# Head loads on one queue, q tiles and normaliser spread over the state stage, folded Wo written group by group

## The chip, the cores and the metric

One core of one Trainium2 chip. The metric is the time of one execution in device microseconds; "span" is the profiled part of one profiled execution, about 1.7 us shorter. TensorE is called PE (its weight loads PEld), VectorE DVE, ScalarE ACT, SyncE (which issues the DMAs) SP, GpSimd POOL.

## The reference

Linear attention with 32 heads of 20 channels over 2048 tokens, model width 640, then an output projection:

```python
qkv = (x @ wqkv) -> q, k, v            # x 2048x640, wqkv 640x1920, bf16
phi = lambda t: where(t > 0, t + 1, exp(t)) + 1e-6
kv  = einsum("bhsd,bhse->bhde", phi(k), v)
z   = einsum("bhsd->bhd", phi(k))
num = einsum("bhqd,bhde->bhqe", phi(q), kv)
den = einsum("bhqd,bhd->bhq", phi(q), z)[..., None] + 1e-6
out = (num / den) @ wo
```

The kernel never forms v. It accumulates the state P = x^T phi(k), makes kv = wv^T P per head, and folds kv into Wo: W2 = blockdiag(kv) Wo. Then out = (phi(q) / den) W2, one matmul chain for each of 16 token tiles.

## The kernel before

The stages on PE, in order: a **head** (loads, transposes of the first x tiles), **k** (16 token tiles, then phi(k)), the **state** (two halves of 16 steps), then a **late stage** (kv, six "w2 groups" that make W2, most q tiles, den and its spread, the normaliser), then the **output** tiles. Here den makes the denominators of a block of four token tiles, the spread brings their inverses to the columns of phi(q), and the normaliser multiplies phi(q) by them. W2 comes out of its matmuls with rows grouped by head, while the output matmuls need it in another row order. This kernel brings the rows to other partitions by DMA, so W2 makes a round trip: copied to SBUF (`w2g`), written to a DRAM scratch (`w_rows`), read back as `w2p`. No output matmul can start before all of `w2p` is there.

```python
        def w2_rows():
            P.add("sp", lambda e: e.dma_start(
                w2d[0:5 * GW, :].rearrange("(g p) n -> p g n", p=GW),      # GW = 120
                w2g[0:GW, 0:5 * D].rearrange("p (g n) -> p g n", n=D)),
                reads=[("w2g", g) for g in range(5)], writes=["w2d"], dma=True)
            P.add("sp", lambda e: e.dma_start(
                w2d[5 * GW:D, :], w2g[0:gsz[5], 5 * D:6 * D]), ...)
            for c in range(NC_):                                           # 5 reads, 128 partitions each
                P.add("sp", lambda e, c=c: e.dma_start(
                    w2p[:, c * D:(c + 1) * D],
                    w2d.rearrange("(h c j) n -> c h j n", c=NC_, j=4)[c]),
                    reads=["w2d", "w2d5"], writes=[("w2p", c)], dma=True)
...
        for h in range(2):                       # state: 3 q tiles in each half
            for st in range(NT):
                p_step(h, st)
                ...
                if st == 7:
                    next_q(5 + qi[0] % 3)
            p_out(h)
            next_q(5 + qi[0] % 3)
            next_q(5 + qi[0] % 3)
        ...
        kv_group(0)                              # late stage: 14 q tiles
        next_q(5)
        z_finish(4)
        w2_group(0, 2)
        next_q(6)
        w2_group(1, 0)
        den(0, 4)
        ...                                      # a q tile between any two w2 groups
        w2_group(5, 0)
        den(1, 4)
        w2_rows()
        ...                                      # 8 more q tiles, den and normaliser of blocks 1 and 2
        for st in range(2):
            out_tile(st)
        ...
```

A q tile is five matmuls on PE (1.085 us), then one ACT instruction and two DVE instructions; its PSUM bank is free after the last of these.

## Time and profile before

| | before |
|---|---|
| median of the first runs (range) | 109.37 us (109.25 to 109.81) |
| span of the profiled run | 107.7 us |
| PE busy | 92% |
| PE waits over 0.2 us, all together | 4.9 us |
| first w2 group to first output matmul | 61.3 to 81.0 us: 19.7 us |
| `w2p` complete (landing record of the last read) | 79.7 us |

The page of the profile: span, busy shares, PE's busy tenths in 40 slices, and the clock granted to PE in the same slices (9 is full).

```profile
span 107.7 us, 1890 instructions
PE 99.6 (92%) x749; PEld 64.8 (60%) x755; DVE 68.2 (63%) x136; ACT 41.3 (38%) x77; POOL 10.7 (10%) x27
PE   5899999999799999999999999985999879999990
PEclk9999999999999999999999999999999999999999
```

PE is busy nearly everywhere: the kernel is bound by the matmuls, and there is little to win but the holes. The four longest waits of PE by releaser (total us, times, longest) name them:

```profile
PE ps L323 <- DVE pq L336: 1.5, 1, 1.5
PE ps L261 <- DVE eps L155: 1.3, 1, 1.3
PE ps L482 <- ACT rd L466: 0.7, 1, 0.7
PE ps L297 <- DVE pk L288: 0.7, 1, 0.7
```

L323 is a q tile waiting for a PSUM bank, L297 the first state matmul waiting for the banks of the k tiles, L482 an output tile waiting for the PSUM bank from which ACT copies the last spread. In the timeline of PE and of SP (start, duration, engine, line, operation, what ended the idle time before it) the round trip looks like this:

```profile
61.32 0.46 PE L413 MATMUL ps<-wog,kvt 120*120 120x320 bf16 x2
...
71.89 0.39 PE L462 MATMUL ps<-rdc,em 128*128 128x128 bf16 x4
73.80 3.41 PE L323 MATMUL ps<-xT,wqp 128*128 128x512 bf16 x14 [1.52 <-DVE pq L336]
...
81.00 2.88 PE L482 MATMUL ps<-w2p,pq 128*128 128x320 bf16 x20
```

```profile
68.91 0.34 SPq L423 DMA_DIRECT2D w_rows<-w2g  x1
70.25 0.29 SPq L427 DMA_DIRECT2D w_rows<-w2g  x1
74.43 3.16 SPq L431 DMA_DIRECT2D w2p<-w_rows  x5
```

The five reads again, with the starts of the first and the last, and then the page's line of their median time to landing (last figure, us):

```profile
L431 SPq DMA_DIRECT2D w2p<-w_rows x5: 587/603/604, 74.4 to 77.0; - x5
w2p<-w_rows SPq DMA_DIRECT2D x5, 160.0 KB, 2.7
```

The writes are issued at 68.9 and 70.3, the reads from 74.4, the last read lands at 79.7. So the trip takes 10.8 us from the first write's issue and 18.4 us from the first w2 group (61.3). PE spends 19.7 us on the w2 groups and other work (waits of 1.5 us included) before it wants W2, and L482 starts at 81.0 without a wait. There are 1.3 us to spare.

### The profile page before, as it was taken

What the parts mean: (1) busy time and instruction counts of PE and PEld (TensorE: products, weight loads), DVE (VectorE), ACT (ScalarE), POOL (GpSimd) and SP (SyncE); (2) the same over time, 40 slices, a digit from 0 to 9 for tenths busy, and PEclk for the clock granted to TensorE, in tenths of its full rate; (3) what the DMA queues carried; (4) which work ended last, traced back from release to release, by engine and by line L of the source; (5) the groups of instructions that cost most, each with busy time, mean ns of one, the idle gap of its engine ahead of it and who ended that gap; (6) DMA issues with size and microseconds to landing.
All of it is one profiled execution on the core that took longest, in us unless ns stands there. A gap on an engine that the chain in (4) does not pass through costs nothing.

```text
span 107.7 us, 1890 instructions
## 1 busy us (share of the span) xinstructions
PE 99.6 (92%) x749; PEld 64.8 (60%) x755; DVE 68.2 (63%) x136; ACT 41.3 (38%) x77; POOL 10.7 (10%) x27
## 2 busy tenths in 40 slices
PE   5899999999799999999999999985999879999990
PEld 2467777777476674676767745432446557777760
DVE  1216998888899899701236674999879583333331
ACT  0404555555500206202035289872665433333330
POOL 6881000191000000000000000000000000000000
PEclk9999999999999999999999999999999999999999
DMA  2998999999980000000000000082730222333333
GB/s 52 370 203 190 223 145 213 383 366 363 266 161 0 0 3 0 0 0 6 0 0 3 0 0 6 14 215 75 194 111 0 85 104 85 119 117 125 118 120 115
DMA packets 16330, 12.24 MB, mean 114 GB/s; under 512 B 8386, under 2 KB 16322, under 8 KB 16322
## 3 DMA queue, kind: packets, MB, share of 16 engines
q1 hardware_dynamic: 15602, 11.31, 38.6%
q10 hardware_dynamic: 720, 0.82, 2.2%
q8 instruction: 6, 0.10, 0.4%
q14 instruction: 2, 0.02, 0.1%
HBM read 6.72 MB, written 3.44 MB: 94 GB/s over the span
## 4 chain that ended last, share of the span: by engine, by line
PE 75%; DVE 13%; ACT 5%; DMA 3%; issue 1%
PE ps L270 19%; PE ps L482 18%; PE ps L297 15%; PE ps L323 15%; DVE za L342 4%; DVE pq L336 3%; DMA xn<-in_x_dram 3%; ACT eq L331 3%; PE ps L199 2%; DVE pq L473 2%; PE ps L441 2%; PE ps L392 1%; DVE eq L333 1%; ACT rd L466 1%; PE ps L373 1%
## 5 line engine op out<-in xcount | busy, mean ns | idle before, releaser
L323 PE MATMUL ps<-xT,wqp 128*128 128x512 bf16 x94 | 22.9, 379 | 1.8 <-DVE pq L336 1.5
L297 PE MATMUL ps<-pk,xn 128*128 128x320 bf16 x160 | 22.4, 299 | 0.8 <-DVE pk L288 0.7
L482 PE MATMUL ps<-w2p,pq 128*128 128x320 bf16 x160 | 22.2, 299 | 0.7 <-ACT rd L466 0.7
L270 PE MATMUL ps<-wk,xT 128*128 128x320 bf16 x160 | 22.3, 299 | 0.0
L297 PEld LDWEIGHTS ps<-pk,xn 128*128 128x128 bf16 x160 | 15.5, 98 | 7.9 <-DVE pk L288 1.0
L331 ACT ACTIVATE eq<-ps 128x512 bf16<-128x512 f32 x20 | 11.9, 597 | 21.4 <-PE ps L323 21.3
L482 PEld LDWEIGHTS ps<-w2p,pq 128*128 128x128 bf16 x160 | 15.5, 98 | 7.0 <-ACT rd L466 0.8
L270 PEld LDWEIGHTS ps<-wk,xT 128*128 128x128 bf16 x160 | 15.7, 98 | 6.4 <-issue 0.6
L283 ACT ACTIVATE ek<-ps 128x640 bf16<-128x640 f32 x16 | 11.2, 704 | 13.5 <-PE ps L270 13.5
L323 PEld LDWEIGHTS ps<-xT,wqp 128*128 128x128 bf16 x100 | 9.3, 98 | 11.0 <-DVE pq L336 1.9
L491 DVE CAST osb<-ps 128x320 bf16<-128x320 f32 x16 | 7.8, 490 | 11.5 <-PE ps L482 11.5
L336 DVE SCALAR_TENSOR_TENSOR pq<-ps,eq 128x512 bf16<-128x512 f32 x20 | 13.8, 692 | 0.7
L288 DVE SCALAR_TENSOR_TENSOR pk<-ps,ek 128x640 bf16<-128x640 f32 x16 | 13.2, 825 | 0.5
L333 DVE TENSOR_SCALAR eq<-eq 128x512 bf16<-128x512 bf16 x20 | 5.8, 292 | 10.9 <-ACT eq L331 10.4
L489 ACT CAST osb<-ps 128x320 bf16<-128x320 f32 x16 | 6.8, 426 | 13.2 <-PE ps L482 13.1
L473 DVE TENSOR_TENSOR pq<-pq,rd 128x512 bf16<-128x512 bf16 x20 | 7.0, 418 | 0.3 <-ACT rd L466 0.3
L285 DVE TENSOR_SCALAR ek<-ek 128x640 bf16<-128x640 bf16 x16 | 5.4, 335 | 1.7 <-ACT ek L283 1.6
L203 DVE COPY xT<-ps 128x640 bf16<-128x640 bf16 x4 | 2.0, 492 | 6.7 <-PE ps L199 6.6
L309 ACT CAST pt<-ps 128x320 bf16<-128x320 f32 x6 | 2.2, 434 | 9.7 <-PE ps L297 9.7
L342 DVE TENSOR_TENSOR za<-pk 128x1280 f32<-128x1280 bf16 x4 | 5.7, 1484 | 0.0
L253 POOL COPY wqp<-wqn 128x640 bf16<-128x640 bf16 x5 | 3.7, 773 | 12.6 <-DMA wqn<-in_wqkv_dram 12.6
L261 PE MATMUL ps<-zero 128*128 128x512 bf16 x7 | 3.4, 630 | 1.3 <-DVE eps L155 1.3
(40 smaller groups left out, 47.6 us busy)
## 6 DMA issues: line engine op xcount, KB each, us to landing
out_dram<-osb SPq DMA_DIRECT2D x16, 160.0 KB, 1.8
xn<-in_x_dram SPq DMA_DIRECT2D x3, 640.0 KB, 7.7
wqn<-in_wqkv_dram SPq DMA_DIRECT2D x1, 800.0 KB, 5.3
wv<-in_wqkv_dram SPq DMA_DIRECT2D x1, 800.0 KB, 10.7
w2p<-w_rows SPq DMA_DIRECT2D x5, 160.0 KB, 2.7
wog<-in_wo_dram SPq DMA_DIRECT2D x1, 750.0 KB, 13.0
w_rows<-w2g SPq DMA_DIRECT2D x1, 750.0 KB, 5.3
wk<-in_wqkv_dram ACTq DMA_DIRECT2D x3, 160.0 KB, 3.9
```

The costliest lines, as they stand in the source:

```text
L270: r = e.matmul(bank(b + h, HALF), xT[:, c * S + 128 * st:c * S + 128 * st + 128], wk[:, c * D + HALF * h:c * D + HALF * (h + 1)], start=(c ...
L283: P.add("act", lambda e: e.activation(fold(t[:, :]), two_banks(b), ACTF.Exp), reads=banks + ["table"], writes=[("ek", st % 3)])
L288: P.add("dve", lambda e: e.scalar_tensor_tensor(fold(pk[:, st * D:(st + 1) * D]), two_banks(b), 0.0, fold(t[:, :]), ALU.max, ALU.add), rea ...
L297: r = e.matmul(bank(d, HALF), xn[:, st * D + 128 * d:st * D + 128 * d + 128], pk[:, st * D + HALF * h:st * D + HALF * (h + 1)], start=(st ...
L323: r = e.matmul(bank(b), wqp[:, d * D + 128 * c:d * D + 128 * c + 128], xT[:, d * S + BK * sbk:d * S + BK * (sbk + 1)], start=(d == 0), sto ...
L331: P.add("act", lambda e: e.activation(t[:, :], bank(b), ACTF.Exp), reads=[("bank", b), "table"], writes=[("eq", i)])
L333: P.add("dve", lambda e: e.tensor_scalar(t[:, :], t[:, :], 1.0, 1e-6, ALU.min, ALU.add), reads=[("eq", i)], writes=[("eq", i)])
L336: P.add("dve", lambda e: e.scalar_tensor_tensor(pq[:, c * S + BK * sbk:c * S + BK * (sbk + 1)], bank(b), 0.0, t[:, :], ALU.max, ALU.add), ...
L342: P.add("dve", lambda e: e.tensor_tensor(d_ap, a, b, ALU.add), reads=ra + rb, writes=[dst])
L473: P.add("dve", lambda e, v=v: e.tensor_tensor(v, v, rd[i][:, :], ALU.mult), reads=[("rd", i), ("pq", sbk, c)], writes=[("pq", sbk, c)])
L482: r = e.matmul(bank(b + h, HALF), pq[:, c * S + 128 * st:c * S + 128 * st + 128], w2p[:, c * D + HALF * h:c * D + HALF * (h + 1)], start=( ...
L491: P.add("dve", lambda e: e.tensor_copy(osb[j][:, HALF:D], bank(b + 1, HALF)), reads=[("bank", b + 1)], writes=[("osb", j, 1)])
```

## The change

Its intent: close the holes, and start the round trip early. (1) The head's nine small loads go out on one queue in the order of need, and the first k tiles are worked block by block. (2) The state starts on four banks instead of five. (3) Six more q tiles, z, and den and spread of block 0 move into the state stage, where DVE is idle; normaliser multiplies go one to a q tile instead of in blocks of five. (4) kv's columns are put in the order that `w2p` needs while they are masked; each w2 group is copied half by ACT and half by DVE and written as soon as it is copied, and all six writes are queued ahead of six reads. With (1), the first DMA transpose of x no longer waits for the first load of wk.

```diff
-            for eng, what in (("act", "x0 w0 w2 w4 x2"), ("sp", "x1 w1 w3 x3")):
+            for k in "x0 w0 x1 w1 w2 w3 w4 x2 x3".split():      # all on "sp"
...
+        def w2_write(g):
+            w = gsz[g] // NC_
             P.add("sp", lambda e: e.dma_start(
-                w2d[0:5 * GW, :].rearrange("(g p) n -> p g n", p=GW),
-                w2g[0:GW, 0:5 * D].rearrange("p (g n) -> p g n", n=D)),
+                w2d.rearrange("(c r) n -> c r n", c=NC_)[:, 24 * g:24 * g + w, :],
+                w2g[0:gsz[g], g * D:(g + 1) * D]), ...)
+        def w2_read(g):
+            w = gsz[g] // NC_
             P.add("sp", lambda e: e.dma_start(
-                    w2p[:, c * D:(c + 1) * D],
-                    w2d.rearrange("(h c j) n -> c h j n", c=NC_, j=4)[c]),
+                w2p[24 * g:24 * g + w, :].rearrange("p (c n) -> p c n", n=D),
+                w2d.rearrange("(c r) n -> r c n", c=NC_)[24 * g:24 * g + w]), ...)
... (state stage: next_q() after steps 3, 6, 9, 12 of the first half, 1, 5, 8, 11 of the second)
+        kv_group(0)
+        small[:] = [5, 6, 7, 4]
+        next_q()
+        for g in range(NG):
+            w2_group(g, 2 * ((g + 1) % 2))
+            w2_write(g)
+            if g == 1:
+                inverse(1)
+            if g in (1, 3):
+                next_q()
+        for g in range(NG):
+            w2_read(g)
+        spread(1)
+        next_q()
+        next_q()
+        inverse(2)
+        next_q()
+        next_q()
+        spread(2)
+        next_q()
+        out_tile(0, 0)
...
```

More of the change, by code (lines that the diff above doesn't have):

```diff
@@ L190, in load_xT @@
                     xT[:, :].rearrange("p (c s) -> p c s", s=S)[:, :, a:b], x[0, a:b, :]),
-                    reads=[("wk", 0)] if i == 0 else [],
                     writes=[("xT", NPE + i)], dma=True)
@@ L223, in load_wk @@
         def load_wk():
-            for eng, what in (("act", "x0 w0 w2 w4 x2"), ("sp", "x1 w1 w3 x3")):
-                for k in what.split():
-                    n = int(k[1])
-                    if k[0] == "x":
-                        load_xn(n, n + 1, eng)
-                    else:
-                        P.add(eng, lambda e, n=n: e.dma_start(
-                            wk[:, n * D:(n + 1) * D],
-                            wqkv[128 * n:128 * n + 128, D:2 * D]), writes=[("wk", n)], dma=True)
+            for k in "x0 w0 x1 w1 w2 w3 w4 x2 x3".split():
+                n = int(k[1])
+                if k[0] == "x":
+                    load_xn(n, n + 1, "sp")
+                else:
+                    P.add("sp", lambda e, n=n: e.dma_start(
+                        wk[:, n * D:(n + 1) * D],
+                        wqkv[128 * n:128 * n + 128, D:2 * D]), writes=[("wk", n)], dma=True)
             tl = mybir.InstLoadActFuncSet(
@@ L291, in k_phi, with p_step @@
                 reads=banks + [("ek", st % 3)], writes=[("pk", st)])
-        def p_step(h, st):
+        def p_step(h, st, ds=range(NC_)):
             def mm(e):
-                for d in range(NC_):
+                for d in ds:
                     r = e.matmul(
@@ L302, in p_step @@
             P.add("pe", mm, reads=[("xn", st), ("pk", st)],
-                  writes=[("bank", d) for d in range(NC_)])
+                  writes=[("bank", d) for d in ds])
         def p_out(h):
@@ L400, in kv_group @@
                       writes=[("bank", bb)])
-            for lo, n, bb, w, key in ((0, 4, b, GW, 0), (4, 1, b + 1, GW, 1), (5, 1, b + 1, 40, 2)):
-                src = ps[0:w, BK * bb + 128 * (lo % 4):BK * bb + 128 * (lo % 4) + 128 * n] \
-                    .rearrange("p (g j) -> p g j", j=128)[:, :, 0:w]
-                mk = bm[0:w, 0:w].unsqueeze(1).broadcast_to([w, n, w])
-                dst = kvt[0:w, GW * lo:GW * (lo + n)].rearrange(
-                    "p (g j) -> p g j", j=GW)[:, :, 0:w]
+            for g in range(NG):
+                bb, w, nh = b + g // 4, gsz[g], gsz[g] // DH
+                src = ps[0:w, BK * bb + 128 * (g % 4):BK * bb + 128 * (g % 4) + w].rearrange(
+                    "p (h c j) -> p h c j", c=NC_, j=4)
+                mk = bm[0:w, 0:w].rearrange("p (h c j) -> p h c j", c=NC_, j=4)
+                dst = kvt[0:w, GW * g:GW * g + w].rearrange("p (c h j) -> p h c j", h=nh, j=4)
                 P.add("dve", lambda e, src=src, mk=mk, dst=dst: e.tensor_tensor(
-                    dst, src, mk, ALU.mult), reads=[("bank", bb), "bm"], writes=[("kvt", key)])
+                    dst, src, mk, ALU.mult), reads=[("bank", bb), "bm"], writes=[("kvt", g)])
         def w2_group(g, b):
@@ L415, in w2_group @@
                     wog[0:n, g * D + HALF * h:g * D + HALF * (h + 1)], start=True, stop=True),
-                    reads=[("kvt", 0 if g < 4 else g - 3), "wog", "wog5"],
+                    reads=[("kvt", g), "wog", "wog5"],
                     writes=[("bank", b + h)])
-            P.add("act", lambda e: e.copy(
-                fold(w2g[0:n, g * D:(g + 1) * D]), two_banks(b, parts=n)),
-                reads=[("bank", b), ("bank", b + 1)], writes=[("w2g", g)])
-        def w2_rows():
-            P.add("sp", lambda e: e.dma_start(
-                w2d[0:5 * GW, :].rearrange("(g p) n -> p g n", p=GW),
-                w2g[0:GW, 0:5 * D].rearrange("p (g n) -> p g n", n=D)),
-                reads=[("w2g", g) for g in range(5)], writes=["w2d"], dma=True)
-            P.add("sp", lambda e: e.dma_start(
-                w2d[5 * GW:D, :], w2g[0:gsz[5], 5 * D:6 * D]),
-                reads=[("w2g", 5)], writes=["w2d5"], dma=True)
-            for c in range(NC_):
-                P.add("sp", lambda e, c=c: e.dma_start(
-                    w2p[:, c * D:(c + 1) * D],
-                    w2d.rearrange("(h c j) n -> c h j n", c=NC_, j=4)[c]),
-                    reads=["w2d", "w2d5"], writes=[("w2p", c)], dma=True)
+            P.add("act", lambda e: e.copy(w2g[0:n, g * D:g * D + HALF], bank(b, HALF, parts=n)),
+                  reads=[("bank", b)], writes=[("w2g", g, 0)])
+            P.add("dve", lambda e: e.tensor_copy(
+                w2g[0:n, g * D + HALF:(g + 1) * D], bank(b + 1, HALF, parts=n)),
+                reads=[("bank", b + 1)], writes=[("w2g", g, 1)])
+        def w2_write(g):
+            w = gsz[g] // NC_
+            P.add("sp", lambda e: e.dma_start(
+                w2d.rearrange("(c r) n -> c r n", c=NC_)[:, 24 * g:24 * g + w, :],
+                w2g[0:gsz[g], g * D:(g + 1) * D]),
+                reads=[("w2g", g, 0), ("w2g", g, 1)], writes=[("w2d", g)], dma=True)
+        def w2_read(g):
+            w = gsz[g] // NC_
+            P.add("sp", lambda e: e.dma_start(
+                w2p[24 * g:24 * g + w, :].rearrange("p (c n) -> p c n", n=D),
+                w2d.rearrange("(c r) n -> r c n", c=NC_)[24 * g:24 * g + w]),
+                reads=[("w2d", g)], writes=[("w2p", g)], dma=True)
         def den(sbk, b):
@@ L467, in den_spread, with normalize, out_tile @@
                   reads=[("bank", b)], writes=[("rd", i)])
-        def normalize(sbk):
+        def normalize(sbk, c):
             i = sbk % 2
-            for c in range(NC_):
-                v = pq[:, c * S + BK * sbk:c * S + BK * (sbk + 1)]
-                P.add("dve", lambda e, v=v: e.tensor_tensor(v, v, rd[i][:, :], ALU.mult),
-                      reads=[("rd", i), ("pq", sbk, c)], writes=[("pq", sbk, c)])
-        def out_tile(st):
-            b = 2 * (st % 4)
+            v = pq[:, c * S + BK * sbk:c * S + BK * (sbk + 1)]
+            P.add("dve", lambda e: e.tensor_tensor(v, v, rd[i][:, :], ALU.mult),
+                  reads=[("rd", i), ("pq", sbk, c)], writes=[("pq", sbk, c)])
+        def out_tile(st, b):
             j = st % 4
@@ L487, in out_tile @@
                 P.add("pe", mm, reads=[("pq", st // 4, c) for c in range(NC_)]
-                      + [("w2p", c) for c in range(NC_)], writes=[("bank", b + h)])
+                      + [("w2p", g) for g in range(NG)], writes=[("bank", b + h)])
             P.add("act", lambda e: e.copy(osb[j][:, 0:HALF], bank(b, HALF)),
@@ L504, in bass_standalone__linear_attn_block__prompt_kernel @@
         transpose_x(0, 6)
-        transpose_x(1, 7)
-        warm(2)
-        for c in range(NC_):
-            for st in range(2):
+        warm(1)
+        for st, cs in ((0, (0,)), (1, None), (0, (1, 2)), (1, (0, 1, 2)), (0, (3, 4)), (1, (3, 4))):
+            if cs is None:
+                transpose_x(st, 7)
+                continue
+            for c in cs:
                 for h in range(2):
                     k_half(st, h, (c,))
-            if c >= 3:
-                transpose_x(c - 1, c + 3)
+        transpose_x(2, 6)
+        transpose_x(3, 7)
         for st in range(2):
@@ L520, in bass_standalone__linear_attn_block__prompt_kernel @@
         qs = [(s, c) for s in range(NSB) for c in range(NC_)]
-        qi = [0]
-        def next_q(b):
-            q_tile(*qs[qi[0]], b)
-            qi[0] += 1
-        for h in range(2):
-            for st in range(NT):
-                p_step(h, st)
-                if zst and st % 2 == 1:
-                    zst.pop(0)()
-                if st == 7:
-                    next_q(5 + qi[0] % 3)
-            p_out(h)
-            next_q(5 + qi[0] % 3)
-            next_q(5 + qi[0] % 3)
-        for f in zst:
-            f()
@@ L539, in bass_standalone__linear_attn_block__prompt_kernel @@
-        kv_group(0)
-        next_q(5)
-        z_finish(4)
-        w2_group(0, 2)
-        next_q(6)
-        w2_group(1, 0)
-        den(0, 4)
-        den_act(0, 4)
-        next_q(7)
-        w2_group(2, 2)
-        den_spread(0, 4)
-        next_q(5)
-        w2_group(3, 0)
-        normalize(0)
-        next_q(6)
-        w2_group(4, 2)
-        next_q(7)
-        w2_group(5, 0)
-        den(1, 4)
-        w2_rows()
-        den_act(1, 4)
-        next_q(5)
-        next_q(6)
-        den_spread(1, 4)
@@ L563, in bass_standalone__linear_attn_block__prompt_kernel @@
-        normalize(1)
-        while qi[0] < 15:
-            next_q((7, 2, 3, 5, 6)[qi[0] % 5])
-        next_q(0)
-        next_q(1)
-        den(2, 4)
-        den_act(2, 4)
-        next_q(2)
-        next_q(3)
-        den_spread(2, 4)
-        normalize(2)
-        next_q(5)
-        for st in range(2):
-            out_tile(st)
-        den(3, 6)
-        den_act(3, 6)
-        out_tile(2)
-        den_spread(3, 6)
-        normalize(3)
-        for st in range(3, NT):
-            out_tile(st)
+        todo = []
@@ new lines, in bass_standalone__linear_attn_block__prompt_kernel, with take, next_q, inverse @@
+        small = [5, 6, 7]
+        def take():
+            small.append(small.pop(0))
+            return small[-1]
+        def next_q(n=1):
+            q_tile(*qs.pop(0), take())
+            for _ in range(n):
+                if todo:
+                    todo.pop(0)()
+        def inverse(sbk):
+            b = take()
+            den(sbk, b)
+            den_act(sbk, b)
+        def spread(sbk):
+            den_spread(sbk, take())
+            todo.extend(lambda c=c: normalize(sbk, c) for c in range(NC_))
@@ new lines, in bass_standalone__linear_attn_block__prompt_kernel @@
+        p_step(0, 0, range(4))
+        p_step(0, 1, range(4))
+        p_step(0, 0, (4,))
+        p_step(0, 1, (4,))
+        for st in range(2, NT):
+            p_step(0, st)
+            if st % 3 == 2:
+                zst.pop(0)()
+            if st in (3, 6, 9, 12):
+                next_q()
+        p_out(0)
+        next_q()
+        next_q()
+        for st in range(NT):
+            p_step(1, st)
+            if st in (0, 2, 4):
+                zst.pop(0)()
+            if st == 7:
+                z_finish(take())
+            if st == 9:
+                inverse(0)
+            if st == 12:
+                spread(0)
+            if st in (1, 5, 8, 11):
+                next_q()
@@ new lines, in bass_standalone__linear_attn_block__prompt_kernel @@
+        assert not zst
+        p_out(1)
+        next_q()
+        next_q()
+        kv_group(0)
+        small[:] = [5, 6, 7, 4]
[6 more added lines that the diff above has]
+            if g in (1, 3):
+                next_q()
+        for g in range(NG):
+            w2_read(g)
+        spread(1)
+        next_q()
+        next_q()
+        inverse(2)
+        next_q()
@@ L585, in bass_standalone__linear_attn_block__prompt_kernel @@
+        next_q()
+        spread(2)
+        next_q()
+        out_tile(0, 0)
+        for f in todo[:2]:
+            todo.pop(0)()
+        out_tile(1, 2)
+        while todo:
+            todo.pop(0)()
+        inverse(3)
+        out_tile(2, 0)
+        out_tile(3, 2)
+        small[:] = [7]
+        spread(3)
+        for st in range(4, NT):
+            out_tile(st, 2 * (st % 4) if st > 5 else 2 * (st % 2))
+            if todo:
+                todo.pop(0)()
         block = es(nc.Block())
```

## The prediction

> **What bounds it now.** TensorE. The page has PE busy 92% of 107.7 us and its waits hold only 4.9 us. Spacing in the timeline: k and state and output matmuls 0.136 us each, a q tile (5 matmuls) 1.085, kv 1.63, z 1.04. Summed, dense work is about 95 us. The rest: head to the first transpose 4.0 us, tail after the last matmul about 3 us, and holes. Holes in the timeline: 0.8 us before the first state matmul (it waits for the k tile that holds bank 4), 0.3 between the state halves, 1.6 at 72.1 us (q waits for a bank behind a block of five normaliser multiplies on DVE), 0.5 and 0.8 around the last den and spread.
>
> **State stage.** Starting on banks 0-3 covers the 0.8; moving z adds away from the copies covers the 0.3. Six q tiles plus z, one den, one spread move from the late stage into this one, where DVE is mostly idle: no PE work is removed. Gain 1.1 us.
>
> **Head.** About zero. x0 alone on the queue should land near 3.3 us instead of 3.9, and k starts near 4.7 instead of 5.9. But the SP issues at about 0.43 us each, so x1 lands near 4.2; the array is still slow (transposes 0.105 us, later 0.056); and x2's transpose now stands just before k tile 2, which waits about 0.5 us for the DVE copy. Dense k still starts near 9.2 us.
>
> **Late stage.** From the end of the state stage to the last output matmul PE took 49.3 us; without the moved work that is 41.1, of which 3.4 are waits. The normaliser and den/spread holes go; DVE gets six masks (about 0.22 us each), half of the w2 copies (0.44 each) and one multiply per q tile. Adding durations in program order, the w2 groups wait about 2 us for DVE.
>
> **Folded Wo.** The write's DRAM side is 5x24x640. The Trainium skill, "DMA: Bandwidth & Descriptors", section on why a DMA increments its semaphore by 16, says the engine count is the largest k up to 16 dividing both slowest dimensions: here 5, always the same five. The trace agrees with the rule: the 40-row write has 11 landing updates (10 engines and one at once), and about 15 were active in the 120-partition write. At 55 ns a 1280-byte packet, one write takes 1.3 us, all six 7 us. Reads cannot be issued until the sixth write is (in order on SP), 0.6 us each, 24 partitions each, on 12 engines. I expect all of w2p some 19.5 to 21 us after the state stage; PE wants it at 17.6. So a new hole of 1 to 4 us, about 2.5, before the first output tile.
>
> **Sum.** -1.1 state, 0 head (+-0.5), late stage about +1 (-0.5 to +3). I predict 109.1 us, range 107.0 to 111.2. Chances: faster by over 2% 0.16, within 0.69, slower 0.15.
>
> **What would show it.** Right: no hole before the first state matmul; q hole at 72 us gone; one hole of 1 to 4 us before the first output matmul ending with the last w2p read; w2 writes landing with 6 updates, about 1.3 us apart; dense k start at 9.2 +-0.5. Wrong: w2p there before PE asks for it (then about 107), or dense k starting before 8.5.
>
> **What would make it wrong.** Writes on more engines: 1 to 2 us faster. Reads into 24 partitions slower than assumed, or a hole long enough to slow the array's clock: 2 us slower.

## The result

| | before | after |
|---|---|---|
| median of 4 runs | 109.55 us | 114.91 us (114.36 to 115.58) |
| ratio | | 1.049 (1.042 to 1.057) |
| span of the profiled run | 107.7 us | 113.8 us |
| first w2 group to first output matmul wanted | 61.3 to 81.0: 19.7 us | 67.8 to 79.9: 12.1 us |
| `w2p` complete | 79.7 us: 18.4 after the first group | 85.1 us: 17.3 after it |

Ratios, here and below, are the mean time of one kernel's runs over the mean of the other's runs of the same rounds, so not quite the ratio of the medians quoted. The page after, with the same lines as before:

```profile
span 113.8 us, 1914 instructions
PE 102.9 (90%) x754; PEld 65.0 (57%) x754; DVE 71.4 (63%) x145; ACT 40.2 (35%) x77; POOL 10.6 (9%) x27
PE   5998999999999999999999999899109999999980
PEclk9999999999999999999999999999975599999999
```

Two things are new: two slices in which PE hardly works (1 and 0), and right behind them slices in which the granted clock is 7, 5, 5 tenths. PE busy rises from 99.6 to 102.9 us although the change adds no matmul: matmuls at half speed count as busy for twice as long (2.6 of the 3.3 us, see a_warm). The waits of PE:

```profile
PE ps L482 <- DMA w2p<-w_rows: 5.2, 1, 5.2
PE ps L259 <- DVE eps L155: 1.3, 1, 1.3
PE ps L268 <- DVE xT L202: 0.6, 2, 0.3
PE ps L412 <- DVE w2g L419: 0.5, 1, 0.5
```

All four waits shown of before are gone except the one at the start (L259 here). In their place stands one wait of 5.2 us, of the first output tile for the reads of W2. In the timeline of PE, and of SP:

```profile
67.79 1.09 PE L412 MATMUL ps<-wog,kvt 120*120 120x320 bf16 x4
...
78.86 1.24 PE L321 MATMUL ps<-xT,wqp 128*128 128x512 bf16 x5
85.36 5.49 PE L482 MATMUL ps<-w2p,pq 128*128 128x320 bf16 x20 [5.25 <-DMA w2p<-w_rows]
90.78 0.47 PE L443 MATMUL ps<-pq,zb 128*32 128x128 bf16 x20
91.18 2.89 PE L482 MATMUL ps<-w2p,pq 128*128 128x320 bf16 x20
```

```profile
70.40 6.07 SPq L426 DMA_DIRECT2D w_rows<-w2g  x6
76.52 4.90 SPq L433 DMA_DIRECT2D w2p<-w_rows  x6
```

The first 20 output matmuls take 5.49 us, the next 20 take 2.89. The chain of waits, in order of time (start, duration, what), shows what the first of them waited for:

```profile
75.77 5.38 DMA w_rows<-w2g
81.14 0.02 issue
81.16 3.96 DMA w2p<-w_rows
85.12 0.24 issue
85.36 5.49 PE ps L482 x20
```

The last write is issued at 75.8 and has landed only at 81.1; the last read can be issued then, and lands at 85.1. The busy time by stretch (the stretch and its length; then PE, PEld, DVE, ACT and POOL busy, granted clock, DMA share, GB/s) gives the last two columns their meaning:

```profile
73.00:77.00 4.00, 4.00 (x40) 1.94 (x41) 3.52 (x9) 2.62 (x6) 0.00 (x0) 1.00 0.33 117
84.00:85.00 1.00, 0.00 (x0) 0.00 (x0) 0.00 (x0) 0.00 (x0) 0.00 (x0) 0.50 0.07 24
88.00:90.80 2.80, 2.80 (x15) 1.32 (x15) 1.16 (x3) 0.43 (x1) 0.00 (x0) 0.50 0.16 59
91.00:93.00 2.00, 2.00 (x34) 1.40 (x23) 1.63 (x5) 1.10 (x3) 0.00 (x0) 1.00 0.22 82
```

While the writes run (73 to 77), a third of 16 DMA engines is busy: 5 engines. And the clock record has PE at half speed from 84.0 to 90.8 us: it fell about 4 us into the hole and rose 5.5 us after work had resumed. That loss varies from run to run: the runs of 115.58 (the profiled one) and 115.32 us had a mean granted clock of 0.970, those of 114.36 and 114.51 us 0.983 and 0.984, at a span about 1 us shorter. As an estimate from these, (1 - 0.983) x 112.7 x 2 makes 3.8 us at half clock there, against 6.8 in the profiled run.

### The profile page after: what moved, and what is told of

Read it like the earlier page. It is cut to its first block, busy times and chain, and to the rows that moved or that the text cites. A ratio compares the mean times of both kernels' runs of the same rounds, so it can differ in the third digit from the quotient of the medians.

```text
span 113.8 us, 1914 instructions
## 1 busy us (share of the span) xinstructions
PE 102.9 (90%) x754; PEld 65.0 (57%) x754; DVE 71.4 (63%) x145; ACT 40.2 (35%) x77; POOL 10.6 (9%) x27
## 4 chain that ended last, share of the span: by engine, by line
PE 79%; DMA 12%; DVE 2%; SPq 2%; ACT 1%; issue 1%
PE ps L482 22%; PE ps L295 19%; PE ps L268 18%; PE ps L321 14%; DMA w_rows<-w2g 5%; DMA wk<-in_wqkv_dram 4%; DMA w2p<-w_rows 3%; SPq L228 2%; PE ps L412 1%; PE ps L390 1%; ACT eq L329 1%; PE ps L443 1%; PE ps L371 1%; SPq L217 1%; PE ps L464 1%
## 5 line engine op out<-in xcount | busy, mean ns | idle before, releaser
L482 PE MATMUL ps<-w2p,pq 128*128 128x320 bf16 x160 | 24.8, 320 | 5.2 <-DMA w2p<-w_rows 5.2
L321 PE MATMUL ps<-xT,wqp 128*128 128x512 bf16 x100 | 24.2, 379 | 0.0
L482 PEld LDWEIGHTS ps<-w2p,pq 128*128 128x128 bf16 x160 | 16.4, 103 | 13.1 <-issue 5.7
L295 PE MATMUL ps<-pk,xn 128*128 128x320 bf16 x160 | 23.9, 299 | 0.0
L268 PE MATMUL ps<-wk,xT 128*128 128x320 bf16 x160 | 22.9, 301 | 0.6 <-DVE xT L202 0.6
L329 ACT ACTIVATE eq<-ps 128x512 bf16<-128x512 f32 x20 | 11.9, 597 | 27.2 <-PE ps L321 27.2
L268 PEld LDWEIGHTS ps<-wk,xT 128*128 128x128 bf16 x160 | 15.2, 98 | 7.9 <-issue 0.8
L489 ACT CAST osb<-ps 128x320 bf16<-128x320 f32 x16 | 6.8, 425 | 19.7 <-PE ps L482 19.6
L286 DVE SCALAR_TENSOR_TENSOR pk<-ps,ek 128x640 bf16<-128x640 f32 x16 | 13.2, 824 | 0.5
L474 DVE TENSOR_TENSOR pq<-pq,rd 128x512 bf16<-128x512 bf16 x20 | 8.1, 417 | 0.0
L283 DVE TENSOR_SCALAR ek<-ek 128x640 bf16<-128x640 bf16 x16 | 6.3, 393 | 1.4 <-ACT ek L281 1.2
L340 DVE TENSOR_TENSOR za<-za 128x1280 f32<-128x1280 f32 x3 | 4.4, 1481 | 0.0
L164 POOL TENSOR_SCALAR_AFFINE_SELECT em<-em 128x128 bf16<-128x128 bf16 x8 | 4.2, 521 | 0.5
```

The source lines that it names most:

```text
L268: r = e.matmul(bank(b + h, HALF), xT[:, c * S + 128 * st:c * S + 128 * st + 128], wk[:, c * D + HALF * h:c * D + HALF * (h + 1)], start=(c ...
L286: P.add("dve", lambda e: e.scalar_tensor_tensor(fold(pk[:, st * D:(st + 1) * D]), two_banks(b), 0.0, fold(t[:, :]), ALU.max, ALU.add), rea ...
L295: r = e.matmul(bank(d, HALF), xn[:, st * D + 128 * d:st * D + 128 * d + 128], pk[:, st * D + HALF * h:st * D + HALF * (h + 1)], start=(st ...
L321: r = e.matmul(bank(b), wqp[:, d * D + 128 * c:d * D + 128 * c + 128], xT[:, d * S + BK * sbk:d * S + BK * (sbk + 1)], start=(d == 0), sto ...
L329: P.add("act", lambda e: e.activation(t[:, :], bank(b), ACTF.Exp), reads=[("bank", b), "table"], writes=[("eq", i)])
L340: P.add("dve", lambda e: e.tensor_tensor(d_ap, a, b, ALU.add), reads=ra + rb, writes=[dst])
```

## The experiments

Three explanations were open. **Theory 1**: the new writes, on 5 engines, make W2 late; the old path would have been in time. **Theory 2**: the trip always took about this long, and the change took away the work that covered it. **Theory 3**: the trip starts late, because DVE copies the groups late and SP issues in order. The first four runs of the table shared one chip and its runs of the kernel before, so did the next four, and the last three.

| run | based on | median us | ratio to before |
|---|---|---|---|
| a_oldfold | after | 115.41 | 1.053 (1.049 to 1.058) |
| a_wide | after | 113.85 | 1.041 (1.036 to 1.046) |
| a_warm | after | 112.78 | 1.029 (1.024 to 1.034) |
| a_cover | after | 109.41 | 0.999 (0.995 to 1.002) |
| b_fold | before | 112.60 | 1.025 (1.020 to 1.030) |
| b_head | before | 110.18 | 1.002 (0.998 to 1.006) |
| a_read | after | 113.11 | 1.030 (1.026 to 1.034) |
| best1 | after | 109.75 | 0.999 (0.995 to 1.004) |
| a_free | after, wrong result on purpose | 108.06 | 0.988 (0.984 to 0.992) |
| best2 | after | 109.59 | 1.000 (0.995 to 1.006) |
| best3 | after | 107.63 | 0.983 (0.979 to 0.987) |

### a_oldfold: the old path of W2 in the new order

```diff
-                dst = kvt[...].rearrange("p (c h j) -> p h c j", ...)   # and src, mk alike
+                dst = kvt[0:w, GW * g:GW * g + w]                        # natural order
-            w2_write(g)                  # after each group
-        for g in range(NG):
-            w2_read(g)
+        w2_rows()                        # as before: two writes, five reads
```

> The changed kernel with the folded Wo written and read back as before (two writes on 15 and 10 engines, then five reads). Theory 1, five-engine writes are what makes w2p late: w2p is there when TensorE asks (79.9 us), no hole, about 107 us. Theory 2, the round trip always took about 10.8 us from the write's issue to the last read (68.9 to 79.7 in the profile of before), and the change took away the q tiles that covered it: write issued near 75.4, w2p near 86, a hole of about 6 us before the first output matmul and again slow output matmuls, 114 to 116 us.

Measured 115.41 us, as theory 2 has it. SP issues the writes at 75.0 and 75.4, the reads from 80.5, and the hole is there:

```profile
78.87 1.24 PE L321 MATMUL ps<-xT,wqp 128*128 128x512 bf16 x5
85.97 4.86 PE L480 MATMUL ps<-w2p,pq 128*128 128x320 bf16 x20 [5.86 <-DMA w2p<-w_rows]
```

The last read lands at 85.9 us, 10.9 us after the first write was issued; before it was 10.8. Theory 1 falls: the old path, unchanged in itself, is as late in the new order: 18.1 us after the first w2 group (67.80), before 18.4. That leaves the order of work on PE; a_cover tests it.

### a_wide: the same writes on more engines

```diff
-                w2d.rearrange("(c r) n -> c r n", c=NC_)[:, 24 * g:24 * g + w, :],
+                w2d[GW * g:GW * g + gsz[g], :],
...             # and the read of group g from its own 120 rows, "(c r) n -> r c n"
```

> The changed kernel with the scratch rows laid out group by group, so each write goes out as 120 rows by 640 (15 engines expected, 16 landing updates) in place of 5x24x640 (5 engines, 6 updates). Theory 1: writes land about 2 us after issue, reads are no longer queued behind them, last w2p at 80 to 81.5, hole 0 to 1.5 us, no slow matmuls: 107 to 109 us. Theory 3, it is only the late issue (DVE copies, SP order) that makes w2p late: the hole stays above 4 us and the time above 113.

Measured 113.85 us: theory 1's expectation missed. Theory 3's was met in its numbers, by little (4.06 us, and 113.85 against 113), but not for its reason. The writes did what was expected: 16 landing updates for each of 120 rows in place of 6, 2.0 us from issue to landing, the last landed at 77.1 us instead of 81.1. But `w2p` was complete only at 83.9, and a wait of 4.06 us was left. Four microseconds gained on the writes gave about 1.3 on the trip, because the reads are slow too. The stretch in which the six 24-partition reads run, and then the stretch of the five 128-partition reads in the kernel before:

```profile
78.00:81.00 3.00, 2.17 (x14) 0.91 (x11) 2.89 (x9) 2.09 (x4) 0.00 (x0) 1.00 0.84 152
```

```profile
76.00:79.00 3.00, 3.00 (x32) 1.35 (x32) 2.67 (x6) 1.94 (x5) 0.00 (x0) 1.00 0.88 245
```

The DMA engines are as busy (0.84 and 0.88), and move 152 GB/s against 245. The 1280-byte packets of the narrow reads took 105 ns in this stretch (median; half of them 92 to 131), against a median of 55 ns. In the changed kernel, where the reads go out one by one as the slow writes land, their median was 62 ns between 81.2 and 84.9 us: the half pace did not show there.

### a_warm: matmuls of zeros in the hole

```diff
+        for _ in range(22):
+            P.add("pe", lambda e: e.matmul(
+                bank(2), zero[:, 0:128], zero[:, :], start=True, stop=True),
+                reads=["zero"], writes=[("bank", 2)])
         out_tile(0, 0)
```

> The changed kernel with 22 matmuls of zeros (4.75 us) before the first output tile, into a free bank. If the array's clock drops in the hole and the first 20 output matmuls pay for it (0.272 against 0.136 us each), w2p still lands near 85.1 but the output matmuls run at 0.136 from the start: 112.2 us (111.5 to 112.9). If the slow matmuls come from something else (w2p or pq reads), the time stays near 114.9.

Measured 112.78 us, as expected of a clock effect. The last read landed at 84.5, and the output tiles behind it run at full speed:

```profile
79.87 4.91 PE L596 MATMUL ps<-zero 128*128 128x512 bf16 x21
84.62 2.88 PE L482 MATMUL ps<-w2p,pq 128*128 128x320 bf16 x20
```

So the hole costs twice: its length, and then 2.6 us in the traces (20 matmuls at 0.267 instead of 0.136 us). That matmuls of zeros, which contribute nothing to the result, make the kernel 2% faster (1.049 to 1.029) shows that the clock was the second loss. (The two ratios are from different chips, each against the kernel before on its own.)

### a_cover: four q tiles moved back behind the w2 groups

```diff
-            if st in (3, 6, 9, 12):            # state, first half
+            if st in (3, 9):
-            if st in (1, 5, 8, 11):            # second half
+            if st in (1, 5):
...         # inverse(1) after group 3; three more next_q() before inverse(2), one more after spread(2)
```

> The changed kernel with four q tiles (4.3 us of TensorE) taken out of the state stage and put between the last w2 group and the first output tile. No work is added or removed and the DMAs stay as they are. Theory 2 (cover) says the hole shrinks from 5.2 to about 1 us and the array stays fast: 107 to 109 us. If the reads are late relative to the q tiles (theory 1 alone, DVE-bound), the hole stays over 3 us and the time over 111.

Measured 109.41 us, 0.4 above the range expected. The hole is gone (0.3 us of wait is left at the first output tile), with the DMAs left as they were, five-engine writes and narrow reads included: `w2p` complete at 81.8, first output matmul at 82.0. The timeline of PE and of SP:

```profile
79.60 2.11 PE L321 MATMUL ps<-xT,wqp 128*128 128x512 bf16 x9
82.00 2.88 PE L482 MATMUL ps<-w2p,pq 128*128 128x320 bf16 x20 [0.29 <-issue]
```

```profile
66.02 6.95 SPq L426 DMA_DIRECT2D w_rows<-w2g  x6
73.02 3.42 SPq L433 DMA_DIRECT2D w2p<-w_rows  x6
```

The trip took 18.4 us from the first w2 group (63.4), a little more than in the changed kernel, and was covered. This is the clearest result for theory 2: the same work in another place takes the loss away. It doesn't reach below the kernel before, because with the q tiles back in the late stage PE waits for DVE there: 1.8 us at the two den steps.

### a_free: no round trip at all (wrong result on purpose)

```diff
-        for g in range(NG):
-            w2_read(g)
...             # in load_rest: w2p[:, c * D:(c + 1) * D] <- wo[128 * c:128 * c + 128, :]
```

> Wrong result on purpose: the changed kernel with w2p loaded from Wo at the start, so that no output matmul depends on the round trip; the w2 groups, their copies and their six writes stay, the reads back are gone. This is what the change is worth without the hole. If the hole and the slow clock behind it are the whole loss, the span of 113.8 falls by 5.2 and 2.7 to about 105.9: 107.5 us (106.6 to 108.4). If the other parts of the change cost as well (w2 groups waiting for DVE, head), 109 or more.

Measured 108.06 us, inside the range of the first expectation. The span is 106.3 us, and output starts with no wait:

```profile
78.96 1.24 PE L325 MATMUL ps<-xT,wqp 128*128 128x512 bf16 x5
80.04 2.88 PE L486 MATMUL ps<-w2p,pq 128*128 128x320 bf16 x20
```

This splits the result. Everything else in the change is worth 1.4 us (107.7 to 106.3 in span, 1.2% in time). The round trip costs 7.5 us of span (106.3 to 113.8): the wait of 5.2 and the half clock's 2.6 make 7.8. The rest is mostly behind the last matmul, where a_free has 3.6 us to the end of the span and the changed kernel 3.2.

### b_fold and b_head: two parts of the change alone

b_fold puts the changed masks, split copies, `w2_write` after each group and `w2_read` after the last into the kernel before, and leaves its q tiles alone. b_head takes the changed head alone.

```diff
+        w2_group(0, 2)
+        w2_write(0)
...                          # b_fold: so for each group; then, in place of w2_rows():
+        for g in range(NG):
+            w2_read(g)
```

```diff
-            for eng, what in (("act", "x0 w0 w2 w4 x2"), ("sp", "x1 w1 w3 x3")):
+            for k in "x0 w0 x1 w1 w2 w3 w4 x2 x3".split():
...                          # b_head: and the order of the first transposes and k blocks
```

> The kernel before with the changed folded-Wo path alone (six masks, copies split over ACT and DVE, six five-engine writes, six 24-partition reads), its q tiles left where they were. If the cause is the lost cover and not the path, there is no hole before the first output matmul: 109.5 us (108.8 to 110.3). If the path by itself costs, w2p comes after 81 us and the time is 112 or more.

> The kernel before with the changed head alone (one queue, strict order, block-wise first tiles). The trace of the changed kernel has the dense k stretch start at 9.61 us against 9.19: 109.9 us (109.5 to 110.3). If the head is a gain that other parts hid: 109.0 or less.

b_fold: 112.60 us. In its numbers this is the second expectation (`w2p` complete at 82.05, the time over 112), though no wait for `w2p` made the time: PE came to the output only at 84.0. There is no hole before the output, as theory 2 says, but partly by luck, since PE had been delayed; the trip itself took 20.2 us from the first w2 group (61.8), against 18.4. The loss came elsewhere. DVE now has six masks and half of the copies to do in the stretch where the q tiles already waited for it: the wait for a bank, 1.5 us before, became 2.09, and that gap was enough for the clock to fall. The clock record has it at half from 75.4 to 78.8 us. The timeline of PE:

```profile
72.64 0.39 PE L465 MATMUL ps<-rdc,em 128*128 128x128 bf16 x4
75.11 5.10 PE L323 MATMUL ps<-xT,wqp 128*128 128x512 bf16 x15 [2.09 <-DVE pq L336]
```

In the kernel before, the 14 recorded matmuls of the same three q tiles took 3.41 us, here 15 take 5.10. So the path alone isn't free: its trip was 1.8 us longer here, and its DVE work becomes PE time where q tiles already waited for DVE. In the changed kernel the multiplies no longer stand there in a block of five, and no q tile waits.

b_head: no difference (1.002). One queue issues a load every 0.47 us; in the trace of the changed kernel the weight loads of k waited 0.7 us for wk.

### a_read and best1: wider reads

a_read orders the rows inside a group as (h j c), so that a write goes out as 24x5x640 on 12 engines (13 landing updates), and reads `w2p` back in pieces of 96 and 32 partitions. best1 adds the old head, and puts the ACT and DVE part of the two q tiles between the w2 groups behind the w2 copies.

```diff
-                dst = kvt[...].rearrange("p (c h j) -> p h c j", h=nh, j=4)
+                dst = kvt[...].rearrange("p (h j c) -> p h c j", h=nh, j=4)
-        for g in range(NG):
-            w2_read(g)
+        w2_read(0, 4)
+        w2_read(4, 6)
```

```diff
+            if g in (1, 3):                  # best1, in the loop of the groups
+                late.append(q_tile(*qs.pop(0), take()))      # matmuls only
+        for f in late:
+            f()                              # ACT and DVE part
```

> The changed kernel with the rows of each group ordered so that a write goes out as 24x5x640 (12 engines), and w2p read back in two pieces of 96 and 32 partitions in place of six of 24. Theory 4, reads into 24 partitions run at half pace (packets of 100 to 138 ns in the run with wide writes, against 55 ns in the 128-partition reads of before): packets at 55 ns, w2p complete near 81, hole 0.5 to 2 us, no slow matmuls, 107.8 to 109.5 us. If the second half of the round trip is slow for another reason (reading rows just written), w2p comes after 83 and the time stays above 112.

> The run before this one with the head of the kernel before, and with the ACT and DVE part of the two q tiles between the w2 groups put after the w2 copies, so that the writes are issued earlier. w2p near 78 to 79 and wanted near 79, no hole, array fast throughout: span about 105, 106.7 us (105.8 to 108). If w2p is still the limit, a hole of over 1 us stays and the time is 108 or more.

a_read: 113.11 us, a miss. The reads do move more: 270 GB/s at a DMA share of 1.05 between 80.5 and 83 us, against 152. But each of the two waits for more writes, SP needs about 0.75 us to issue each of these writes (0.32 for those of a_wide), the masks, now storing single bf16 elements 10 bytes apart, take 0.63 us each (median) against 0.27 and make a w2 group wait 0.6 us, and this run's k stretch also lost time to the DMA transposes of x, so PE came to the output later. `w2p` was complete at 84.1, with 2.4 us of wait and the half clock again. That wide reads alone cure the trip isn't shown. best1, 109.75 us, has a wait of 0.7 us left, no slow clock, and three waits for DVE and ACT around the w2 groups (0.45 to 0.76 us): no better than before.

### best2 and best3: towards a version that beats both

best2 takes the state stage of the change, the old head, natural row order, six contiguous writes of 120 rows, the five old reads, best1's delayed q parts, and moves two q tiles behind the w2 groups. best3 moves those two tiles back, puts den of block 1 ahead of kv and its spread behind the groups, puts off the first multiplies, and lets ACT copy the even groups whole.

```diff
+                w2d[GW * g:GW * g + gsz[g], :], w2g[0:gsz[g], g * D:(g + 1) * D]),      # best2, best3
...
+        next_q(0)                           # best3
+        next_q(0)                           # two q tiles without a multiply
+        inverse(1)
+        kv_group(0)
+        late = [q_tile(*qs.pop(0), take())]
+        for g in range(NG):
+            w2_group(g, 2 * ((g + 1) % 2))
+            w2_write(g)
+            if g in (1, 3):
+                late.append(q_tile(*qs.pop(0), take()))
+                late.pop(0)()
+        w2_reads()
```

> A version built from the findings: state stage and late stage of the change, head and row order of the kernel before, six contiguous writes of 120 rows (15 engines, SP issue 0.44 us each), five 128-partition reads as before, the two q tiles between the w2 groups finished after the w2 copies, and two q tiles moved back from the state stage to behind the w2 groups. Writes landed near 75.5, reads done near 81, wanted near 81: no hole or under 0.5 us, array fast, span 105.2, 107.0 us (106.0 to 108.3). If the round trip still needs more cover than that, a hole of over 1 us and 108.5 or more.

> The run best2 had w2p at 78.6 us, 3 us before it was wanted, and lost 2.6 us in waits of TensorE for ACT and DVE around the w2 groups and the den of block 1. Here the two q tiles go back to the state stage (12 there), block 1's den goes ahead of kv, its spread behind the w2 groups, the first multiplies are put off until after the w2 copies, and ACT copies the even groups whole. If the round trip is about 11 us after the first w2 group and is covered, and the waits are gone: span about 104.3, 106.0 us (105.0 to 107.6). If DVE bounds this stretch whatever the order, 107.6 or more.

best2: 109.59 us, a miss. `w2p` was there at 78.6, three microseconds before it was wanted: the trip is no longer the limit, DVE is (1.5 us of waits of q tiles, 0.7 of a w2 group). best3: 107.63 us, correct, 1.7% faster than the kernel before (the interval of the ratio, 0.979 to 0.987, lies below 1, but a gain of 2% is not certain); just outside the range expected, at the bound named for the case that DVE limits this stretch. Its waits of PE over 0.2 us, complete:

```profile
PE ps L261 <- DVE eps L155: 1.3, 1, 1.3
PE ps L489 <- DVE pq L481: 1.0, 1, 1.0
PE ps L323 <- DVE pq L339: 0.6, 1, 0.6
PE ps L199 <- DMA xn<-in_x_dram: 0.5, 1, 0.5
```

The first output tile (L489) now waits 1.0 us for a normaliser multiply; the last read landed at 80.4, just before the tile's start at 80.7. The trip took 11.9 us from the first w2 group. So DVE came last here, but the read only 0.3 us before: a faster DVE alone would win no more than that at this tile.

Theory 3 was not tested alone; it may have a share. The last write was issued 8.0 us after the first w2 group in the changed kernel, 5.7 in best2 and 5.1 in best3, where ACT and DVE parts of q tiles stand behind w2 copies; the trips took 17.3, 12.8 and 11.9 us. The form of writes and reads changed as well, so what the earlier issue gave stays open.

## Why the prediction was wrong

The forecast was 109.1 us, "within" the most likely; measured were 114.9. The mechanism was named, and its size was too small.

- **State stage, -1.1 us: right.** The hole of 0.8 us before the first state matmul and the 0.3 between the halves are gone (at most 0.1 us is left of either).
- **Head, zero: right in time.** b_head gave 1.002. The dense k stretch started at 9.61 us, within the 9.2 +-0.5.
- **Late stage waits for DVE: right in kind.** From the start of kv to the point where the first output tile is wanted, PE took 14.9 us (65.07 to 79.94) for 13.2 us of work, added up from the durations of before; 2 us were foreseen. The hole of q tiles at 72 us is gone.
- **Five engines: right.** The Trainium skill, "DMA: Bandwidth & Descriptors", in the section on why a DMA increments its semaphore by 16, has the rule. The trace agrees: 6 landing updates for a 5x24x640 write, 16 for a 120x640 one, and a DMA share of 0.33 while only writes run.
- **"I expect all of w2p some 19.5 to 21 us after the state stage; PE wants it at 17.6. So a new hole of 1 to 4 us, about 2.5": this step failed.** The state stage ended at 62.9 us; `w2p` came 22.2 us after that and was wanted at 17.0, so the hole was 5.2. Against the middle of the forecast, PE was 0.6 us early and W2 about 2 us late. The term that was too small is the tail of the trip: "all six 7 us" became 10.7 us from the start of the first write (70.4) to the landing of the last (81.1), and the last read, which waits for that landing and not only for the issue, took 4.0 more. The first four writes landed 1.3 to 1.4 us apart, as worked out, but the fifth came 2.6 us after the fourth, once reads were running beside it. The read of group 0 was issued at 76.5 and landed at 81.9, after the last write. The same page of the skill, "Queues, rings and completion order", says that each engine takes the descriptors of a queue in order. The trace fits: of the 12 engines of that read 7 had finished by 79.3 us, and the other five, as many as the writes use, from 80.6 to 81.9.

  What slowed the fifth write stays open. The last write landed 5.4 us after its issue here, 4.8 in a_warm, with the same writes and reads, and 4.3 in a_free, without reads, and only here did the fifth come so late (1.6 us after the fourth in a_warm, 1.7 in a_free). Even in a_free, with no read beside them, the six writes took 9.6 us from the first start to the last landing, so the 7 us was too small whatever the reads did.
- **The half clock: named as a risk, left out of the sum.** "a hole long enough to slow the array's clock: 2 us slower" was 2.6 us in the trace, and a_warm shows its cause. The skill, "TensorE: Matmul & The Clock Gate", Part 1, has a free-running window of 4096 cycles at 1.2 GHz, 3413 ns, and half clock after an idle window. The trace agrees with the length: the half-clock stretches were 6.83 us here, twice that window, and 3.41 us in b_fold. With a wait forecast up to 4 us, its cost belonged into the central figure.

The two terms (2.7 us of hole, 2.6 us of clock) make 5.3 of the 6.5 us by which the profiled run (115.58) missed the forecast; the median missed it by 5.8. The dense k stretch, 0.4 us later than before, and the tail behind the last matmul (3.2 us, before 2.8) make most of the rest. Beyond the sum, the prediction explained the hole by the form of the writes and reads; a_oldfold and a_cover show that the form mattered less than the cover. Before, 19.7 us of PE time stood over a trip of 18.4. After, the trip was 17.3, a microsecond shorter, and the PE time over it 12.1. Moving q tiles to where DVE was idle removed no PE work, so it could gain only holes; what it took away was the time that PE could spend while W2 was under way.

Open: why the narrow reads run at half pace. It was seen in three runs while no writes were under way (a_wide 152 GB/s, b_fold 143, a_cover 140, at DMA shares of 0.83 to 0.84), and wider reads moved more, but partitions, row order and engine count all changed together.

## What to carry to other kernels

Before moving work off a stretch, ask what latency that work was hiding: write down, for each round trip, its length and the PE work that stands over it, and keep the difference positive. In a kernel bound by matmuls, moving matmuls can only gain holes, and it can open one elsewhere. Price a new PE hole of about 2 us or more (2.1 was enough in b_fold, 1.5 in the kernel before was not) at its length plus the cost of a half-clock stretch behind it, and ask of each DMA how many engines and partitions its outermost dimension gives it, for the read as well as for the write.

## What the Trainium skill lacked or had wrong

- "TensorE: Matmul & The Clock Gate", Part 1, gives the half clock after at least one idle window of about 3.4 us. Here it fell after less: in b_fold around a gap of 2.1 us (PE idle until 75.1, half clock from 75.4), in a_read about 2.3 us into the hole (81.8 to 84.1). Gaps of 1.2 us (a_cover) and 1.5 us (before) left it at full.
- "DMA: Bandwidth & Descriptors", Issuing engines are not separate DMA queues, calls the time on the sequencer to start a DMA usually small relative to the DMA itself. On SP a DMA of 120x640 rows took 0.32 us to issue, one of 5x24x640 about 0.70 (landing 3.6 to 5.7 us after its start), one of the old reads 0.60; the changed kernel's six writes and the six reads behind them (0.36 each) are 6.5 us of issue alone, in a trip of 17.3.
- No page puts a number on writing rows to DRAM scratch and reading them back. Here it took 10.8 us from the issue of the first write to the landing of the last read for 800 KB, 10.2 to 10.7 in the best runs (best2, best3).
